# The second routing begun in the last attention steps, and three of 43 expert blocks put under a condition

## The chip, the cores and the metric

One core of one Trainium2 chip runs the whole program in one launch. The metric is the device time of that core in microseconds (us); lower is better. The engines are named as in the profile: PE (TensorE matmul), PEld (its weight loads), DVE (VectorE), ACT (ScalarE), POOL (GpSimd), SP (SyncE).

## The reference

Random-feature attention over 64 heads, and then a mixture of experts in which each token goes to one expert:

```python
B, H, S, Dh = 8, 8, 576, 64           # M = 128 features
proj = x @ omega.T                     # of q and of k
phi  = concat(cos(proj), sin(proj)) / sqrt(M)
kv, z = phi_k.T @ v, sum(phi_k)
attn = (phi_q @ kv) / clamp(phi_q @ z)
x = attn as (N = 4608 tokens, D = 512)
logits = normed(x) @ normed(expert_emb).T / tau   # E = 8 experts
e = argmax(logits); g = softmax(logits)[e]
out[token] = g * (relu(x[token] @ w1[e]) @ w2[e]) # w1 512x1024, w2 1024x512
```

The inputs are the same draw each time. For that draw the argmax sends 1155, 712, 0, 1151, 438, 576, 574 and 2 tokens to the eight experts. Rounded up to blocks of 128 tokens of one expert these are 10 + 6 + 0 + 9 + 4 + 5 + 5 + 1 = 40 blocks. For any input the number is at most 4608 / 128 + 7 = 43, and the kernel before works through 43 blocks always.

## The kernel before, in words

**Attention.** 32 steps n, each one batch and a pair of heads. All engines' queues are written by hand in one loop (the function below the helpers, `for n in range(NS + 1)`), so each engine runs its instructions in the order of the program text. A step n projects and turns into waves the features of k (two steps ahead) and q, sums k features on POOL (`zsum`), multiplies with v, and `num` and `norm` of step n - 1 give rows of x, which go to DRAM (`store_rows`) together with logit sums on POOL (`sums`).

**Routing.** Tokens stand as 36 slots of 128 partitions, 9 slots for a group of two batches. `choose(g)` finds each token's expert on DVE as a one-hot `eq`; `scan` and the two matmuls of `rank` number the tokens of each expert; `starts`, `places` and `places2` make of it a block number and a row in the block; `block_hot` and `row_hot` make one-hots of both, and `invert` (one matmul for a slot) turns them into a list of token numbers by block, which `rows_of` writes as the gather's indices `prm`. `block_experts` gives each block's expert (`eblk`), which PE reads into a register for its weights' addresses.

The first routing (steps 18 to 28) covers the batches 0 to 3 and gives K1 = 11 blocks. The second covers all 36 slots and gives blocks 11 to 42. It can start only when the last attention step has ended, and is spread over blocks j = 0 to 7 by `route_second` (DVE) and `route_second_pe` (PE): `choose` and `scan` at j = 0, `rank` and `starts2` at 1, `places` at 2, `block_hot` at 3, two `row_hot` at 4 and 5 (18 slots each), `invert` and `rows_of` at 6, `block_experts` at 7. A token's number is split there into two parts (`tok_hi`, `tok_lo`), since it doesn't fit in bf16, so `block_hot` has two products and `invert` a right side of 64 columns.

**Blocks.** In iteration j PE runs `hidden(j + 1)` (32 matmuls, L893), then what the routing has for it, then `turn_x(j + 2)` (four transposes, L852) and `result(j)` (8 matmuls of 512 columns, L914). `power` (POOL), `score` and `weigh` (DVE) and `tanh` (ACT) make a block's gate weight. POOL also casts x (`cast`, L806) and issues the scatter of block j (L927) and the gather of block j + 5 (L774). Up to block 7 ACT does PE's evictions alone; later DVE takes a part.

Of the kernel before, what the change touches and what calls it, by code (L numbers as in the profile page):

```python
# [28 lines left out]
def kernel(  # L29
# [19 lines left out]
    P = 128  # L49
# [70 lines left out]
    tok_hi = persist.tile([P, NSLOT], BF16)  # L120
    tok_lo = persist.tile([P, NSLOT], BF16)
    io_p = persist.tile([P, P], BF16)
    io_k = io_p[:, 0:NBLK]
    io_kf = persist.tile([1, NBLK], FP32)
    pref = persist.tile([P, E], BF16)
    tri = persist.tile([P, E, E], FP32)
# [9 lines left out]
    with tc.tile_pool(name="psA", bufs=1, space=PSUM) as psA, tc.tile_pool(  # L136
# [272 lines left out]
        ti = tmpi[:, P : P + NSLOT]  # L409
# [163 lines left out]
        def set_up_routing(n):  # L573
# [6 lines left out]
            elif n == 3:  # L580
                nc.vector.tensor_scalar(ti, tok_i, 63, None, ALU.bitwise_and)
                nc.vector.tensor_copy(tok_lo, ti)
            elif n == 4:
                nc.vector.tensor_scalar(ti, tok_i, 6, None, ALU.arith_shift_right)
                nc.vector.tensor_scalar(tok_hi, ti, 1, None, ALU.add)

        class Arena:
# [3 lines left out]
            def take(self, n, dtype=FP32):  # L591
# [8 lines left out]
                return r if dtype == FP32 else r.bitcast(dtype)[:, 0:n]  # L600

# [59 lines left out]
        def starts2(rk, ns, ar):  # L661
            nc.vector.tensor_copy(sm[:, T0], rk[:, :, ns])
# [7 lines left out]
            nc.vector.tensor_tensor(sm[:, T0], sm[:, T0], sm[:, B1], ALU.subtract)  # L670
            nc.vector.tensor_scalar(sm[:, DOFF], sm[:, T0], float(P), None, ALU.mult)
# [11 lines left out]
        def places2(w, ge, ns, ar):  # L683
            dest = ar.take(ns)
            lo = ar.take(ns, BF16)
            blk = ar.take(ns, BF16)
# [11 lines left out]
        def block_hot(blk, ns, k0, nk, ar):  # L698
            bm = ar.take(ns * nk, BF16).rearrange("p (s k) -> p s k", k=nk)
            rr = ar.take(ns * nk * 2, BF16).rearrange("p (s t k) -> p s t k", t=2, k=nk)  # L700
# [8 lines left out]
        def row_hot(oh, lo, a, b):  # L709
            shp = [P, b - a, P]  # L710
            nc.vector.tensor_tensor(  # L711
# [482 lines left out]
```

## Time and profile before

| what | us |
|---|---|
| median of 3 runs | 521.59 (521.36 to 522.46) |
| the profiled execution, whole | 520.67 |
| its span in the trace | 518.9 |
| attention, to the first matmul of block 0 | 325.5 |
| block 1's first matmul to block 13's (iterations j = 0 to 11) | 331.16 to 395.13 |
| block 13's first matmul to block 42's | 395.13 to 505.00 |
| last scatter issued by | 512.4 |

All numbers of the trace are of the one profiled execution. Busy shares are means over stages with different limits, so stages are read one by one: in the windows table a line is one stretch, with the busy time of each engine in it, the clock that PE was granted (1.00 is full), and what the DMAs moved. A wait is put down to the event that ended it. Line numbers (L893) are those of the kernel before.

### The profile page before, as it was taken

The page shows a single profiled execution, that of the slowest core. Times are in us where ns is not written, and L with a number is a line of the kernel's source. Part 1 is how long each engine was busy: PE and PEld are TensorE (multiplying, and loading weights), DVE is VectorE, ACT ScalarE, POOL GpSimd, SP SyncE. Part 2 cuts the span into 40 slices and gives each one's busy share as a digit, 9 for nine tenths or more (in the row PEclk, how much of TensorE's full clock was granted, in tenths as well). Part 3 has the DMA queues.
Part 4 walks back from the last instruction along what each step waited for, and adds up shares of the span by engine and source line. Part 5 has one row for each costly group of instructions (what it writes and reads, how often), then busy time and mean ns, then how long its engine had stood idle before and what let it go on. Part 6 is the DMA issues. An engine that isn't in the chain of part 4 may idle for free. (4 is left out here: it accounts for less than half of the span.)

```text
span 518.9 us, 19723 instructions
## 1 busy us (share of the span) xinstructions
PE 467.8 (90%) x8073; PEld 381.5 (74%) x8073; DVE 364.6 (70%) x968; ACT 342.9 (66%) x490; POOL 397.4 (77%) x529
## 2 busy tenths in 40 slices
PE   5389999999999999999999988869589999999993
PEld 4378888888887888778888776746457777777771
DVE  2647997677877778879888685569676666666671
ACT  2358988887887887878887775637355554554541
POOL 3549999888787887787778789447768888888872
PEclk9679999999999999999999999989899999999997
DMA  6035899988987988987998876732233334334210
GB/s 188 0 92 135 168 221 193 201 181 195 185 185 178 199 186 170 177 194 161 193 196 167 180 150 134 143 109 97 70 124 124 127 111 136 125 113 150 79 53 1
DMA packets 59113, 75.11 MB, mean 145 GB/s; under 512 B 11398, under 2 KB 38022, under 8 KB 59024
## 3 DMA queue, kind: packets, MB, share of 16 engines
q0 software_dynamic: 19680, 35.83, 34.0%
q1 hardware_dynamic: 39040, 37.93, 27.6%
q8 instruction: 65, 1.06, 0.8%
q14 instruction: 24, 0.20, 0.1%
q10 hardware_dynamic: 304, 0.08, 0.1%
HBM read 73.42 MB, written 20.88 MB: 182 GB/s over the span
## 5 line engine op out<-in xcount | busy, mean ns | idle before, releaser
L893 PEld LDWEIGHTS <-w_sb 128*128 x1376 | 81.0, 98 | 13.4 <-issue 4.2
L893 PE MATMUL ps<-qr,w_sb 128*128 128x128 f16 x1376 | 84.5, 220 | 2.8 <-DVE qr L195 1.7
L914 PE MATMUL ps<-w_sb,cok 128*128 x344 | 82.8, 384 | 0.0
L350 PE MATMUL ps<-kv,siq 128*64 128x73 f32 x1152 | 77.0, 229 | 0.3 <-issue 0.3
L350 PE MATMUL ps<-kv,coq 128*64 128x73 f32 x1152 | 75.5, 226 | 1.4 <-ACT coq L275 1.1
L350 PEld LDWEIGHTS ps<-kv,siq 128*64 128x64 f32 x1152 | 59.4, 135 | 12.2 <-issue 11.2
L287 POOL TENSOR_TENSOR zt<-sik 128x384 f32<-128x384 f32 x32 | 37.0, 1155 | 40.6 <-ACT sik L275 35.2
L774 POOL DMA_INDIRECT xin_all<-rf_x,prm x43 | 47.0, 1093 | 19.6 <-issue 16.3
L350 PEld LDWEIGHTS ps<-kv,coq 128*64 128x64 f32 x1152 | 60.5, 137 | 1.6 <-ACT coq L275 1.2
L263 DVE SCALAR_TENSOR_TENSOR cok<-cok,ps 128x1152 f32<-128x1152 f32 x31 | 42.0, 1354 | 21.7 <-ACT kT L218 20.2
L914 PEld LDWEIGHTS <-cok 128*128 128x128 f16 x344 | 33.2, 99 | 31.6 <-issue 1.6
L228 PE MATMUL ps<-omT,kT 64*128 64x128 f32 x576 | 48.6, 297 | 3.8 <-DVE coq L263 3.5
L275 ACT ACTIVATE cok<-cok,pio 128x1152 f32<-128x1152 f32 x31 | 38.9, 1255 | 17.9 <-DVE cok L269 17.9
L810 ACT ACTIVATE qT<-xin_all 128x512 f16<-128x512 f32 x43 | 27.0, 628 | 31.8 <-DMA xin_all<-rf_x,prm 31.6
L228 PEld LDWEIGHTS ps<-omT,kT 64*128 64x128 f32 x576 | 41.3, 198 | 8.2 <-DVE coq L263 4.3
L263 DVE SCALAR_TENSOR_TENSOR coq<-coq,ps 128x1152 f32<-128x1152 f32 x32 | 43.1, 1346 | 5.0 <-ACT coq L259 5.0
L241 PE MATMUL ps<-qT,omT 32*128 32x288 f32 x512 | 40.6, 431 | 3.2 <-DVE kvT L310 3.0
L275 ACT ACTIVATE siq<-coq 128x1152 f32<-128x1152 f32 x32 | 37.3, 1165 | 8.6 <-DVE coq L263 4.0
L275 ACT ACTIVATE coq<-coq,pio 128x1152 f32<-128x1152 f32 x32 | 40.2, 1256 | 2.7 <-DVE coq L269 2.5
L300 PE MATMUL ps<-sik,v 64*64 64x128 f32 x576 | 36.8, 281 | 5.2 <-DVE coq L263 5.2
L288 POOL TENSOR_TENSOR zt<-zt,sik 128x384 f32<-128x384 f32 x32 | 38.9, 1217 | 2.5
L275 ACT ACTIVATE sik<-cok 128x1152 f32<-128x1152 f32 x31 | 35.8, 1156 | 5.9 <-PE ps L300 5.7
(210 smaller groups left out, 1211.5 us busy)
## 6 DMA issues: line engine op xcount, KB each, us to landing
w_sb<-in_moe_w_dram POOLq DMA_DIRECT2D x32, 512.0 KB
qr<-in_q_dram SPq DMA_DIRECT2D x64, 144.0 KB, 5.2
rf_x<-xb SPq DMA_DIRECT2D x32, 288.0 KB, 6.0
kr<-in_k_dram SPq DMA_DIRECT2D x58, 144.0 KB, 4.0
v<-in_v_dram SPq DMA_DIRECT2D x32, 144.0 KB, 4.2
xin_all<-in_v_dram SPq DMA_DIRECT2D x30, 144.0 KB, 6.9
w_sb<-in_k_dram SPq DMA_DIRECT2D x6, 144.0 KB, 2.8
xin_all<-rf_x,prm POOLq DMA_INDIRECT x43
```

The costliest lines, as they stand in the source:

```text
L228: nc.tensor.matmul(kreg[:, KS[c] * P : KS[c] * P + P], lhsT=t[r0 : r0 + 64, j * P : j * P + P], rhs=omT2[r0 : r0 + 64], start=True, stop=True,
L241: nc.tensor.matmul(qreg[:, g // 2, QW * (g % 2) : QW * (g % 2) + QW], lhsT=omT4[r0 : r0 + 32, b], rhs=t[r0 : r0 + 32].rearrange("p (c b j) ...
L263: nc.vector.scalar_tensor_tensor(out=dst, in0=dst, scalar=CMAGIC, in1=src, op0=ALU.subtract, op1=ALU.subtract)
L275: nc.scalar.activation(st[n][which + nm], t, AF.Sin, bias=pio2 if which == "co" else 0.0, scale=-TWO_PI * SINSC,)
L287: nc.gpsimd.tensor_tensor(zt, t[:, 0:3], t[:, 3:6], ALU.add)
L288: nc.gpsimd.tensor_tensor(zt, zt, t[:, 6:9], ALU.add)
L300: nc.tensor.matmul(kvreg[64 * half : 64 * half + 64, hh], lhsT=d["v"][r0 : r0 + 64, 64 * c : 64 * c + 64], rhs=ph[r0 : r0 + 64, s * P : s ...
L350: nc.tensor.matmul(nm[r0 : r0 + 64, c], lhsT=ph[:, 2 * QW * hh + 64 * c : 2 * QW * hh + 64 * c + 64], rhs=d["kv"][:, hh, half], start=(hal ...
L774: ins = nc.gpsimd.indirect_dma_start(out=t, out_offset=None, in_=x_rows[:], in_offset=bass.IndirectOffsetOnAxis(ap=prm[:, j : j + 1], axis=0),
L810: nc.scalar.activation(late("qT", j % 2, D), xin[j].bitcast(FP32)[:, 0:D], AF.Square, accum_out=gsc[:, j % 4, 0:1],)
L893: nc.tensor.matmul(h_ps[:, f * P : f * P + P], lhsT=weights(k), rhs=d["xT"][:, c * P : c * P + P], start=(c == 0), stop=(c == 3),)
L914: nc.tensor.matmul(y_ps, lhsT=d["hT"][:, c * P : c * P + P], rhs=weights(NW1 + c), start=(c == 0), stop=(c == NW2 - 1),)
```

## The change

1. **Ranks and one-hots early.** The groups 0 to 2 (27 of the 36 slots) are ranked in attention: `scan` on DVE at the end of step 29 and `rank` on PE right behind it; `places_a`, `places_b` and the row one-hot of group 0 at the end of step 30; the row one-hots of groups 1 and 2 at the end of step 31. Row and place don't depend on the last group, only the offset of a block of the second part does. The last group's rank, places and one-hot follow at j = 1 and 2.
2. **A new form of the places.** `pick` multiplies a table of 8 values by `eq` and sums over the experts; offset and block number come for all 36 slots from one `pick` at j = 2. Blocks' order on DVE: `route_second(j)` stands ahead of `score` and `weigh` for j > 0.
3. **One token code.** Token number + 0x400, read as the bits of an fp16 number, replaces the two parts: `block_hot` has one product instead of two, `invert` 32 columns instead of 64, and `rows_of` three DVE instructions instead of four. `invert` and `rows_of` come at j = 5, `block_experts` at j = 6.
4. **Three blocks in a branch.** The loop runs over NMAIN = 40 blocks. `block_experts` also writes the number of blocks (`nbt`); every engine reads it into a register at the end of j = 20, and the last three blocks stand behind `tc.If(nbv > NMAIN)`, one after the other.
5. Buffers: the blocks' hidden rows (`hT`) are in `coq` instead of `cok`, the one-hots in `cok`, and the scratch of the early work in `kT`.

The core of the diff:

```diff
-        def rank(ns, rk):
+        def rank(s0, s1, rk):
+            ns = s1 - s0
             rk = rk[:, 0 : (ns + 1) * E].rearrange("p (e s) -> p e s", e=E)
-            nc.tensor.matmul(rk, lhsT=onesb, rhs=cumx[:, :, 0 : ns + 1], start=True, stop=False)
+            nc.tensor.matmul(rk, lhsT=onesb, rhs=cumx[:, :, s0 : s1 + 1], start=True, stop=False)
             nc.tensor.matmul(
-                rk[:, :, 0:ns], lhsT=sltb, rhs=eq[:, :, 1 : ns + 1], start=False, stop=True
+                rk[:, :, 0:ns], lhsT=sltb, rhs=eq[:, :, 1 + s0 : 1 + s1], start=False, stop=True
             )
             return rk
 
...
+        def slots(s0, s1):
+            return eq[:, :, 1 + s0 : 1 + s1].rearrange("p e s -> p s e")
+
+        def pick(dst, table, s0, s1, ar):
+            t = ar.spare((s1 - s0) * E).rearrange("p (s e) -> p s e", e=E)
+            nc.vector.tensor_tensor(t, table, slots(s0, s1), ALU.mult)
+            nc.vector.tensor_reduce(dst.unsqueeze(2), t, axis=AX.X, op=ALU.add)
+
+        def places_a(rk, s0, s1, ar):
+            ns = s1 - s0
+            d = [ar.take(ns) for _ in range(4)]
+            pick(d[0], rk[:, :, 0:ns].rearrange("p e s -> p s e"), s0, s1, ar)
+            whole(d[1], d[0], -0.49609375)
+            nc.vector.scalar_tensor_tensor(
+                out=p2["lo"][:, s0:s1], in0=d[1], scalar=-float(P), in1=d[0], op0=ALU.mult, op1=ALU.add
+            )
+            return d
+
+        def places_b(d, s0, s1, ar):
+            shp = [P, s1 - s0, E]
+            pick(d[2], bc(sm[:, B1], shp, 1), s0, s1, ar)
+            nc.vector.tensor_tensor(p2["at"][:, s0:s1], d[1], d[2], ALU.add)
+            pick(d[3], bc(sm[:, LIM], shp, 1), s0, s1, ar)
+            nc.vector.tensor_tensor(p2["ge"][:, s0:s1], d[0], d[3], ALU.is_ge)
...
-            nc.vector.tensor_tensor(rr[:, :, 0], bm, bc(tok_hi[:, 0:ns], shp, 2), ALU.mult)
-            nc.vector.tensor_tensor(rr[:, :, 1], bm, bc(tok_lo[:, 0:ns], shp, 2), ALU.mult)
+            nc.vector.tensor_tensor(rr, bm, bc(tokc[:, 0:ns], shp, 2), ALU.mult)
             return rr
...
+                nc.vector.tensor_tensor(
+                    nbt, sm[0:1, ST2, E - 1 : E], sm[0:1, T1, E - 1 : E], ALU.add
+                )
...
+        def early_pe(n):
+            if n == 29:
+                p2["rk"] = rank(0, S3, ROUTE)
+
+        def row_tile():
+            return (
+                pa.tile([P, NCH * P], FP32, tag="cok", name="oh", bufs=2)
+                .bitcast(FP16)
+                .rearrange("p (s m) -> p s m", m=P)
+            )
+
+        def hot(g):
+            s = SG * (g % 2)
+            row_hot(p2["oh"][g // 2][:, s : s + SG], p2["lo"][:, SG * g : SG * g + SG])
+
+        def early_second(n):
+            if n == 29:
+                scan()
+            elif n == 30:
+                ar = p2["ar"] = Arena(pa.tile([P, 5 * P], FP32, tag="kT", name="ar", bufs=1))
+                p2["lo"] = ar.take(NSLOT, FP16)
+                p2["at"] = ar.take(NSLOT)
+                p2["ge"] = ar.take(NSLOT)
+                places_b(places_a(p2["rk"], 0, S3, ar), 0, S3, ar)
+                p2["oh"] = [row_tile()]
+                hot(0)
+            elif n == 31:
+                p2["oh"].append(row_tile())
+                hot(1)
+                hot(2)
...
-                r2["rk"] = r2["a"].take((NSLOT + 1) * E).rearrange("p (e s) -> p e s", e=E)
-                nc.vector.tensor_copy(r2["rk"], r2["ps"])
-                starts2(r2["rk"], NSLOT, r2["a"])
+                starts2(r2["ps"][:, :, SG], r2["a"])
+                d = places_a(r2["ps"], S3, NSLOT, r2["a"])
+                places_b(d, S3, NSLOT, r2["a"])
             elif j == 2:
-                r2["wg"] = places(r2["rk"], NSLOT, r2["a"])
-                r2["blk"], r2["lo"] = places2(*r2["wg"], NSLOT, r2["a"])
+                hot(3)
+                d = r2["a"].take(NSLOT)
+                blk = r2["a"].take(NSLOT, FP16)
+                pick(d, bc(sm[:, DOFF], [P, NSLOT, E], 1), 0, NSLOT, r2["a"])
+                nc.vector.tensor_tensor(d, d, p2["ge"], ALU.mult)
+                nc.vector.tensor_tensor(blk, d, p2["at"], ALU.add)
+                r2["blk"] = blk
             elif j == 3:
                 r2["rr"] = block_hot(r2["blk"], NSLOT, K1, NBLK - K1, r2["a"])
-            elif j == 4:
-                row_hot(r2["oh"][0], r2["lo"][:, 0:18], 0, 18)
             elif j == 5:
-                row_hot(r2["oh"][1], r2["lo"][:, 18:36], 0, 18)
+                rows_of(r2["inv"], K1, NBLK - K1, r2["a"])
             elif j == 6:
-                rows_of(r2["inv"], K1, NBLK - K1, r2["a"])
-            elif j == 7:
                 block_experts(K1, NBLK - K1, True, r2["a"])
...
-        for j in range(NBLK):
+        for j in range(NMAIN):
             eng = "act" if j <= QUIET else "dve"
-            if j + 1 < NBLK:
+            if j + 1 < NMAIN:
                 hidden(j + 1, eng)
             route_second_pe(j)
-            if j + 2 < NBLK:
+            if j > 0:
+                route_second(j)
+            if j + 2 < NMAIN:
                 turn_x(j + 2, eng)
                 power(j + 2)
                 score(j + 2)
-            if j + 3 < NBLK:
+            if j + 3 < NMAIN:
                 cast(j + 3)
                 square(j + 3)
-            if j + 1 < NBLK:
+            if j + 1 < NMAIN:
                 tanh(j + 1)
                 weigh(j + 1)
-            route_second(j)
-            if j + 5 < NBLK and j == 0:
+            if j == 0:
+                route_second(j)
+            if j + 5 < NMAIN and j == 0:
                 gather(j + 5)
             result(j)
-            if j + 5 < NBLK and j > 0:
+            if j + 5 < NMAIN and j > 0:
                 gather(j + 5)
+            if j == 20:
+                nbv = nc.values_load(
+                    nbt[0:1, 0:1], min_val=0, max_val=NBLK,
+                    skip_runtime_bounds_check_because="a count of blocks",
+                )
+
+        with tc.If(nbv > NMAIN):
+            for j in range(NMAIN, NBLK):
+                gather(j)
+            for j in range(NMAIN, NBLK):
+                cast(j)
+                square(j)
+                power(j)
+                score(j)
+                tanh(j)
+                weigh(j)
+                turn_x(j, "dve")
+                expert_of(j)
+                place(j, range(NW1 + NW2))
+                hidden(j, "act")
+                result(j)
```

Left out are the first routing's calls of the changed helpers (`places2` serves it alone now), `row_hot` and `rows_of` with their shorter bodies, and the set-up of the token codes `tokc`. In the changed kernel the row one-hots are at L737, `pick` at L680 and L681, `rows_of` at L750 to L753, a gather at L794, `cast` at L826, `power` at L837, `score` at L843 to L850, `weigh` at L860 to L866, a scatter at L948, the copy of a transposed x at L197, attention's `norm` at L366 to L368, and the branch at L1219.

DVE's queue at the end of step 31, as it was (`gsc` is the scratch of a block's gate, `qr` the transposed x, L364 the first instruction of attention's last `norm`):

```order
L828 TENSOR_SCALAR gsc<-gsc 128x1
L829 RECIPROCAL gsc<-gsc 128x1
L830 TENSOR_SCALAR gsc<-xin_all,gsc 128x8
L195 COPY qr<-ps 128x512
L823 TENSOR_TENSOR ptk<-xin_all,bad 128x1
L827 TENSOR_REDUCE gsc<-xin_all 128x1
```

and as it is now, where `oh` are the row one-hots of the groups 1 and 2:

```order
L848 TENSOR_SCALAR gsc<-gsc 128x1
L849 RECIPROCAL gsc<-gsc 128x1
L850 TENSOR_SCALAR gsc<-xin_all,gsc 128x8
L197 COPY qr<-ps 128x512
L737 TENSOR_TENSOR oh<-io_p,ar 128x1152 x2
L843 TENSOR_TENSOR ptk<-xin_all,bad 128x1
L847 TENSOR_REDUCE gsc<-xin_all 128x1
```

Two row one-hots of 9 slots stand between the copy and the score of block 1.

DVE's queue about iterations 5 and 6 of the blocks, as it was, from a block's `weigh` (L845, L846) to the next block's score:

```order
L845 TENSOR_SCALAR gsc<-gsc 128x1
L846 RECIPROCAL gpos<-gsc 128x1
L711 TENSOR_TENSOR oh<-io_p,xb 128x2304
L823 TENSOR_TENSOR ptk<-xin_all,bad 128x1
L827 TENSOR_REDUCE gsc<-xin_all 128x1
```

and now, ahead of the matching score:

```order
L865 TENSOR_SCALAR gsc<-gsc 128x1
L866 RECIPROCAL gpos<-gsc 128x1
L750 CAST ar<-ps 128x32
L752 TENSOR_SCALAR bad<-ar 128x32
L753 SCALAR_TENSOR_TENSOR prm<-ar,bad 128x32
L843 TENSOR_TENSOR ptk<-xin_all,bad 128x1
```

The one-hot of 18 slots (`oh`, 2304 wide) is gone from here; the inversion's result (`ps`) is read by three DVE instructions an iteration earlier than before.

POOL's queue at the end of the program, as it was (L927 scatters):

```order
L817 TENSOR_TENSOR gsc<-gsc,half_77 128x1
L927 DMA out_dram<-sik,ptk 4608x512
L927 DMA out_dram<-siq,ptk 4608x512
L927 DMA out_dram<-sik,ptk 4608x512
L1189 UNCONDITIONAL_BRANCH
L1189 ISA
```

and now, from the last unconditional scatters on:

```order
L948 DMA out_dram<-sik,ptk 4608x512
L948 DMA out_dram<-siq,ptk 4608x512
L1219 COMPARE_AND_BRANCH
L794 DMA xin_all<-rf_x,prm 128x521 x3
L826 CAST v<-xin_all 128x512
```

The three gathers, casts, powers and scatters of the blocks 40 to 42 now follow the comparison; if it fails, POOL's queue jumps to a second piece of code that ends the same way as the body.

## Rows read from the trace of the kernel before

**Rows 1.** Busy times of the page, and PE in its 40 slices.

```profile
PE 467.8 (90%) x8073; PEld 381.5 (74%) x8073; DVE 364.6 (70%) x968; ACT 342.9 (66%) x490; POOL 397.4 (77%) x529
...
PE   5389999999999999999999988869589999999993
```

**Rows 2.** Windows table, steady blocks: engine busy us (instructions), then clock, DMA share, GB/s.

```profile
395.13:505.00 109.87, 109.34 (x1277) 81.85 (x1276) 72.19 (x378) 57.35 (x143) 92.76 (x116) 1.00 0.36 114
```

**Rows 3.** Windows table, same columns: blocks j = 1, 2, 5, 6, 7 and 8.

```profile
334.90:344.21 9.31, 5.13 (x47) 3.22 (x46) 6.30 (x31) 3.23 (x8) 4.65 (x7) 0.89 0.59 144
344.21:349.45 5.24, 4.59 (x45) 3.48 (x44) 2.85 (x17) 2.42 (x5) 3.22 (x4) 0.86 0.30 95
...
356.94:362.21 5.27, 4.01 (x45) 2.83 (x44) 5.17 (x10) 3.17 (x7) 5.07 (x4) 1.00 0.28 82
362.21:373.95 11.74, 6.45 (x81) 4.71 (x80) 8.64 (x30) 3.28 (x8) 8.67 (x8) 0.85 0.28 92
373.95:378.35 4.40, 3.90 (x45) 2.79 (x44) 1.15 (x10) 2.42 (x5) 2.90 (x4) 1.00 0.20 67
378.35:383.93 5.58, 3.90 (x45) 2.78 (x45) 4.97 (x21) 3.23 (x9) 3.79 (x6) 1.00 0.41 130
```

**Rows 4.** Waits of PE between 331 and 396 us: total, times, longest.

```profile
PE ps L634 <- DVE cumx L630: 4.2, 1, 4.2
PE ps L893 <- DVE qr L195: 1.7, 1, 1.7
PE ps L852 <- POOL v L806: 1.3, 1, 1.3
```

**Rows 5.** Groups by form, 331.16 to 395.13 us: the inversion on PE.

```profile
L718 PE MATMUL ps<-ar,oh 128*128 128x64 bf16 x36 | 1.8, 218 | 5.3 <-DVE oh L711 5.3
```

**Rows 6.** Windows table near the end, same columns; the last is GB/s.

```profile
500.80:504.00 3.20, 3.20 (x43) 2.58 (x42) 2.35 (x14) 1.38 (x3) 2.29 (x4) 1.00 0.11 40
504.00:508.00 4.00, 4.00 (x44) 2.79 (x43) 2.74 (x14) 1.38 (x3) 1.13 (x2) 1.00 0.04 5
508.00:512.00 4.00, 2.40 (x12) 0.88 (x9) 0.95 (x7) 1.37 (x2) 1.56 (x2) 1.00 0.01 0
```

**Rows 7.** Source line L711, row one-hots on DVE: ns min/median/max.

```profile
L711 DVE TENSOR_TENSOR w_sb<-io_p,w_sb x2: 1347/1348/1348, 261.7 to 270.6; 128x1152 bf16<-128x1152 bf16 x2
```

**Rows 8.** Timeline of DVE, second routing: start, us, instruction.

```profile
353.16 0.67 DVE L688 TENSOR_TENSOR xb<-xb,eq 128x288 f32<-128x288 f32 x1
353.86 0.45 DVE L691 TENSOR_REDUCE xb<-xb 128x36 f32<-128x288 f32 x1
...
359.55 1.76 DVE L706 TENSOR_TENSOR ar<-xb,tok_lo 128x1152 bf16<-128x1152 bf16 x1
...
362.99 2.61 DVE L711 TENSOR_TENSOR oh<-io_p,xb 128x2304 bf16<-128x2304 bf16 x1
```

**Rows 9.** Timeline of POOL in the same place.

```profile
364.06 1.96 POOL L817 TENSOR_TENSOR gsc<-gsc,half 128x1 f32<-128x1 f32 x1
```

**Rows 10.** Source line L817, the power on POOL: ns min/median/max.

```profile
L817 POOL TENSOR_TENSOR gsc<-gsc,half x43: 572/584/1960, 323.7 to 503.5; 128x1 f32<-128x1 f32 x43
```

**Rows 11.** Timeline of DVE, steps 30 to 32: idle time before in brackets.

```profile
322.96 0.43 DVE L195 COPY qr<-ps 128x512 f16<-128x512 f16 x1 [5.31 <-PE ps L852]
...
331.30 0.15 DVE L828 TENSOR_SCALAR gsc<-gsc 128x1 f32<-128x1 f32 x1 [2.62 <-POOL gsc L817]
```

**Rows 12.** Timeline of POOL, step 31: the gather of block 3.

```profile
328.99 1.11 POOL L774 DMA_INDIRECT xin_all<-rf_x,prm  x1 [4.63 <-issue]
```

**Rows 13.** Source line L867, register loads on PE: ns min/median/max.

```profile
L867 PEldq TENSOR_LOAD <-eblk x43: 297/301/916, 318.2 to 502.3; - x43
```

**Rows 14.** Source line L1189, the program's end: ns min/median/max, first and last start.

```profile
L1189 SPq EVENT_SEMAPHORE  x11: 17/28/14996, 498.4 to 518.8; - x11
...
L1189 POOLq DRAIN  x3: 51/103/6913, 511.2 to 518.6; - x3
```

**Rows 15.** Timeline of POOL: the last scatter.

```profile
511.40 0.97 POOL L927 DMA_INDIRECT out_dram<-sik,ptk  x1 [0.76 <-ACT sik L926]
```

More of the change, by code (lines that the diff above doesn't have):

```diff
@@ L119 @@
     eblk = persist.tile([1, NBLK], I32)
[L120 to L122 removed]
+    TOK0 = 0x400
+    tokc = persist.tile([P, NSLOT], FP16)
+    nbt = persist.tile([1, 1], I32)
+    io_p = persist.tile([P, P], FP16)
     io_k = io_p[:, 0:NBLK]
@@ L580, in set_up_routing @@
             elif n == 3:
[L581 to L585, printed above, removed]
+                nc.vector.tensor_scalar(tokc.bitcast(I16), tok_i, float(TOK0), None, ALU.add)
         class Arena:
@@ L600, in take, with spare @@
                 return r if dtype == FP32 else r.bitcast(dtype)[:, 0:n]
+            def spare(self, n):
+                if not hasattr(self, "sp"):
+                    self.sp = self.take(n)
+                return self.sp[:, 0:n]
         def bc(ap, shape, axis):
@@ L684, in places2 @@
             dest = ar.take(ns)
-            lo = ar.take(ns, BF16)
-            blk = ar.take(ns, BF16)
+            lo = ar.take(ns, FP16)
+            blk = ar.take(ns, FP16)
             nc.vector.tensor_tensor(w, w, ge, ALU.add)
@@ L727, in rows_of @@
         def rows_of(inv, k0, nk, ar):
[L728 removed]
+            t = ar.take(nk, FP16)
             bd = bad[:, k0 : k0 + nk]
             nc.vector.tensor_copy(t, inv)
[L731 removed]
+            tok = t.bitcast(I16)
+            nc.vector.tensor_scalar(bd, tok, float(TOK0), 200000.0, ALU.is_lt, ALU.mult)
             nc.vector.scalar_tensor_tensor(
[L733 to L737 removed]
+                out=prm[:, k0 : k0 + nk], in0=tok, scalar=-float(TOK0), in1=bd, op0=ALU.add, op1=ALU.add
             )
@@ L910, in result @@
             y_ps = bank(3 + 4 * (j % 2))
-            if j + 2 < NBLK:
+            more = NMAIN if j < NMAIN else 0
+            if j + 2 < more:
                 expert_of(j + 2)
@@ L920, in result @@
                 )
-                if j + 2 < NBLK and c < 6:
+                if j + 2 < more and c < 6:
                     place(j + 2, range(6 * c, min(6 * c + 6, NW1)))
-                if j + 1 < NBLK and c >= 6:
+                if j + 1 < more and c >= 6:
                     place(j + 1, range(NW1 + 6 * (c - 6), min(NW1 + 6 * (c - 5), NW1 + NW2)))
@@ L949, in route_pe @@
             if m == 2:
-                r1["ps"] = rank(S1, ROUTE)
+                r1["ps"] = rank(0, S1, ROUTE)
             elif m == 8:
@@ L1064 @@
                 route_first(n - n1)
+            if not last:
+                early_second(n)
+            early_pe(n)
             if here:
@@ L1091, in route_second_pe @@
             if j == 1:
-                r2["ps"] = rank(NSLOT, bank(6 - 4 * (j % 2)))
-            elif j == 6:
+                r2["ps"] = rank(S3, NSLOT, bank(6 - 4 * (j % 2)))
+            elif j == 5:
                 r2["inv"] = invert(
-                    lambda s: r2["oh"][s // 18][:, s % 18],
+                    lambda s: p2["oh"][s // S1][:, s % S1],
                     r2["rr"], NSLOT, NBLK - K1, bank(6 - 4 * (j % 2)),
@@ L1100, in route_second @@
             if j == 0:
-                oh = [
-                    pa.tile([P, NCH * P], FP32, tag="coq", name="oh", bufs=2)
-                    .bitcast(BF16)
-                    .rearrange("p (s m) -> p s m", m=P)
-                    for _ in range(2)
-                ]
-                r2["oh"] = oh
-                r2["a"] = Arena(
-                    *[
-                        pa.tile([P, NCH, 2 * (W - 1)], FP32, tag="xb", name="xb", bufs=2).rearrange(
-                            "p c w -> p (c w)"
-                        )
-                        for _ in range(2)
-                    ],
-                    pa.tile([P, NCH * P], FP32, tag="cok", name="ar", bufs=2),
+                r2["a"] = Arena(
+                    pa.tile([P, NCH * P], FP32, tag="coq", name="ar", bufs=2),
+                    pa.tile([P, NCH, 2 * (W - 1)], FP32, tag="xb", name="xb", bufs=2).rearrange(
+                        "p c w -> p (c w)"
+                    ),
                 )
+                r2["a"].spare(NSLOT * E)
                 choose(NGRP - 1)
```

52 lines of the change are left out of this document (20 added, 32 removed).

## The prediction

> **What bounds the kernel now.** I read the page's busy shares first: PE is busy 90% of the span, and in the 40 slices its digit is 9 nearly throughout, except for a dip of seven slices a little past the middle [rows 1]. That dip is where attention ends and the second routing runs. So the next view is the windows table, cut at the first matmul of each block's `hidden`. From block 13 to block 42 it shows 29 blocks in 109.87 us, 109.34 of them PE busy at clock 1.00, with POOL at 92.76 as the next busiest [rows 2]. A steady block thus costs 109.87 / 29 = 3.79 us, and PE alone sets it. Against that price I hold the iterations in which the second routing runs [rows 3]. Over 3.79 they lose 5.52 us at j = 1, 1.45 at 2, 1.48 at 5, 7.95 at 6, 0.61 at 7 and 1.79 at 8. PE's waits name the causes: `rank` waits 4.2 us for DVE's scan at j = 1, a transpose waits 1.3 us for POOL's cast at j = 5, and a `hidden` waits 1.7 us for DVE's copy at j = 8 [rows 4]. The groups by form give the one at j = 6: 36 inversion matmuls, 1.8 us busy, stand behind 5.3 us of waiting for the row one-hot L711 [rows 5].
>
> **Three blocks fewer.** First, are there only 40 blocks with tokens? The reference says so for this draw, and the trace agrees. Near the end the DMAs move 40 GB/s x 3.20 us = 128 kB, then 5 x 4.00 = 20 kB, then nothing [rows 6]. A scattered row is 512 x 4 bytes, so 128 kB is 62 rows, the remainder of an expert with 574 = 4 x 128 + 62 tokens. After it comes the block of two tokens, and the last three scatters carry nothing. The comparison fails and three blocks are skipped: 3 x 3.79 = **-11.4 us**. They are the end of the steady stretch, whose work PE does at full clock, so nothing covers them.
>
> **The second routing's stalls.** At j = 6 the wait for the row one-hot goes: the change makes three of four groups in attention and the fourth at j = 2, so the inversion (now at j = 5) waits only for the product of `block_hot`, made at j = 3. The inversion's own 1.8 us [rows 5] stay. That gives 7.95 - 1.8 = 6.15. The 0.61 of j = 7 is the tail of the same jam. The 1.79 of j = 8 is the wait for a copy on DVE [rows 4], queued there behind `block_experts`; the change puts that one iteration earlier, where ACT still evicts alone. Together 6.15 + 0.61 + 1.79 = **-8.5**. I keep the 5.52 of j = 1 (choose and scan of the last group still come after attention and `rank` still waits for them) and the 1.45 of j = 2 and 1.48 of j = 5, since DVE's list work now goes ahead of the gate's work and only moves. Bounds: -4.3 if half of it comes back as waits for DVE at j = 2 to 5, -10.0 if the wait of j = 5 goes too.
>
> **Early work in attention.** Step 29's scan and rank stand where PE later waits for other engines, and I cost them at nothing. If that cover fails, `rank`'s wait delays the queries' projection behind it; the upper bound of this term has room for that. At the end of step 30 DVE gets three `pick` of 216 elements, five short instructions and a row one-hot of 1152, which took 1.35 us in the first routing [rows 7]. A product of 288 took 0.67 and its sum 0.45 [rows 8], so at 216 a pick is an estimated 0.50 + 0.34; with the short ones at 0.15 to 0.2, by the nearest row [rows 11], the sum is 2.5 + 0.9 + 1.35 = 4.8, at most 5.7 with the prices of 288. DVE stood idle 5.31 there [rows 11]. So this costs -0.5 to +0.4: nothing. At the end of step 31 two one-hots (2.70) come ahead of the score of block 1, in an idle stretch of 2.62 [rows 11]: +0.1. What isn't hidden is POOL. While the 18-slot one-hot ran from 362.99 for 2.61 us [rows 8], the power on POOL, started at 364.06, took 1.96 us [rows 9] instead of its median 0.58 [rows 10]. In step 31 the same power, a gather (issue at 328.99) [rows 12] and a cast lie beside the one-hots, and DVE's score waits for that power [rows 11]. I add 1.96 - 0.58 = 1.4 once, and 0.5 for part of the cast's delay (its bound is the 1.35 of one one-hot). Sum: **+2.0**, between 0 and +4 (two slow powers and a whole 1.35).
>
> [...]
>
> **Small edits.** Each of the five engines reads a register at the end of j = 20. The same kind of load for the experts took 0.30 us on PE's queue, 0.92 at most [rows 13]; there are 43 of these now, ahead of work that PE's list already holds. POOL and DVE have 17 and 38 us of slack in the steady stretch [rows 2]. Zero, at most +0.9. A narrower inversion, one product less (1.76 us of DVE [rows 8]) and one DVE instruction less in `rows_of` are off PE's path: zero, and part of the -8.5.
>
> **The end.** Behind block 39 every engine compares and jumps. Before, POOL's last scatter is issued at 511.40 + 0.97 = 512.4 [rows 15], while its final drain takes 6.9 us from 511.2 and SP's last waits reach to the span's end [rows 14]. The jump and one more semaphore instruction come ahead of that drain. No row shows a branch over a body. The nearest short thing is a register load, 0.3 [rows 13]; the far one is the whole drain, 6.9. I take **+1.5**, nearer the short end, since a comparison moves no data and the scatters' landing can hide part; below, 0, since nothing is taken away here but the blocks already counted.
>
> [...]
>
> **Sum.** -11.4 - 8.5 + 2.0 + 0 + 1.5 = -16.4. The profiled execution took 520.67 us (span 518.9, and 1.8 around it), so 504.3; the median of the runs, 521.59, lies 0.9 above that execution, so 505.2. I say **505.0**.
>
> **Rivals.**
> 1. *POOL is held up throughout.* For: the 1.96 us power. Against: the median of 43 is 0.58, so most escape. Every one-hot and product then delays POOL's cast, and PE waits for it as at j = 5. The routing gains only 4.3 and the early work costs 4: 505.2 + 4.2 + 2.0 = 511.4. Chance 0.15.
> 2. *The end costs a second drain.* For: the failing side raises a semaphore after waits on all scatter queues. Against: only one drain of 6.9 stands in the trace. +6.9 in place of 1.5: 510.6. Chance 0.10.
> 3. *Everything pays.* Early work and branch cost nothing and the wait of j = 5 goes: 505.2 - 2.0 - 1.5 - 1.5 = 500.2. Chance 0.10. For it: DVE's idle stretches are long enough.
> 4. *The branch is taken.* If the count that the chip computes is over 40, three blocks run one after another, with gather, cast, transposes and both products in a row and nothing beside them. One such block costs at least 3.79 and at most the 11.74 of the worst iteration [rows 3]; I take twice the steady price, 7.6. Then -11.4 becomes 3 x 7.6 - 11.4 = +11.4: 505.2 + 22.8 = 528.0, slower than before. It decides from 41 blocks on. Against: the byte counts of the last three scatters. Chance 0.02.
>
> **How the numbers follow.** The forecast keeps 0.63, with its own range 501 to 509 from the terms' bounds. A measurement of this kernel can tell about 0.2%, 1.0 us, from no change. Every case but the fourth lies over 10 us below the time before; I leave 0.01 for no change and 0.03 for slower. The range takes in rivals 1 to 3 but for their outer halves: 500 to 511.5.
>
> **What would show it.** In the profile after: steady blocks still near 3.79, and one fewer stretch of three; PE's wait for the inversion gone or under 1 us and the iterations 5 to 8 near 4 to 5.6; `rank` still waiting some 4 us; the first block's start within 2 us of 325.5 and DVE's score of block 1 waiting longer for POOL's power; the time from the last scatter's issue to the span's end, now 518.9 - 512.4 = 6.5, at about 8. The prediction is wrong if the iterations after the second routing keep a wait of 4 us or more, if the end grows by 5 or more, or if 43 blocks still run.

## The result, and the profile after

The changed kernel takes 502.19 us (median of 4 runs, 500.04 to 504.27), the kernel before 521.97 (521.36 to 522.46). The ratio is 0.962 with a 95% interval of 0.957 to 0.967, so 19.8 us are gone where 16.6 were forecast (505.0 against the 521.59 known then). The profiled execution, the shortest of the four, took 500.04 us, with a span of 498.2. Ratios, here and below, leave out runs that lie over 1.5% above the shortest run of the same kernel.

The page of the changed kernel, its busy times and PE in 40 slices:

```profile
PE 454.5 (91%) x7943; PEld 371.9 (75%) x7943; DVE 361.8 (73%) x941; ACT 339.5 (68%) x475; POOL 387.7 (78%) x517
...
PE   5389999999999999999999997895999999999992
```

The dip of seven slices [rows 1] has shrunk to four. The windows table, cut at the first matmul of each block's `hidden`, shows j = 1, 2, 4, 5, 6 and then 25 steady blocks (columns as in [rows 3]; `...` marks left-out lines, here and in every cut below):

```profile
334.80:345.47 10.67, 5.66 (x47) 3.37 (x46) 7.76 (x39) 3.65 (x10) 5.49 (x7) 0.84 0.58 135
345.47:349.21 3.74, 3.74 (x45) 2.79 (x44) 3.43 (x18) 2.97 (x7) 2.25 (x2) 1.00 0.20 74
...
353.44:358.25 4.81, 3.99 (x45) 2.83 (x44) 4.17 (x15) 3.32 (x9) 4.30 (x5) 1.00 0.33 111
358.25:362.89 4.64, 4.64 (x81) 3.69 (x80) 2.08 (x14) 3.19 (x7) 4.11 (x6) 1.00 0.44 148
362.89:366.63 3.74, 3.74 (x46) 2.79 (x44) 3.17 (x14) 2.98 (x7) 2.98 (x5) 1.00 0.46 146
...
389.62:483.63 94.01, 93.80 (x1101) 70.05 (x1100) 63.54 (x330) 51.57 (x126) 79.92 (x100) 1.00 0.39 123
```

The worst iteration of before, 11.74 us at j = 6, is a plain 3.74 now. The inversion stands at j = 5 and PE does not wait for it: the groups by form give 36 matmuls in 1.1 us with no idle time before them (to compare with [rows 5]):

```profile
L742 PE MATMUL ps<-xb,oh 128*128 128x32 f16 x36 | 1.1, 176 | 0.0
```

PE's waits between 331 and 396 us (to compare with [rows 4]):

```profile
PE ps L637 <- DVE cumx L632: 5.0, 1, 5.0
PE ps L872 <- POOL v L826: 1.3, 3, 0.8
```

The wait for a row one-hot and the one for the copy at j = 8 are gone; `rank`'s wait for the scan grew from 4.2 to 5.0, and the iteration j = 1 from 9.31 to 10.67. Between the two profiled executions the account is: first matmul of block 1 -0.1 us (331.16 to 331.06); iterations 1 to 9 -9.7 (52.76 to 43.04); the rest up to the last `hidden` -11.6 (31 iterations in 117.34, 28 in 105.79); behind it +0.6 (13.9 to 14.5). Together -20.7, the difference of the spans.

The source line of the program's end bears on the last of these:

```profile
L1264 POOLq DRAIN  x3: 50/103/5215, 492.1 to 497.9; - x3
```

and the line of the condition, where POOL raises a semaphore ahead of that drain:

```profile
L1219 POOLq COMPARE_BRANCH  x1: 50/50/50, 489.8 to 489.8; - x1
L1219 POOLq INC_SWDGE_SEM  x1: 1447/1447/1447, 490.6 to 490.6; - x1
```

The drain's 6.9 [rows 14] are 1.45 + 5.2 now.

### The profile page after: what moved, and what is told of

Read it like the earlier page. It is cut to its first block, busy times and chain, and to the rows that moved or that the text cites. A ratio compares the mean times of both kernels' runs of the same rounds, so it can differ in the third digit from the quotient of the medians.

```text
span 498.2 us, 19379 instructions
## 1 busy us (share of the span) xinstructions
PE 454.5 (91%) x7943; PEld 371.9 (75%) x7943; DVE 361.8 (73%) x941; ACT 339.5 (68%) x475; POOL 387.7 (78%) x517
## 5 line engine op out<-in xcount | busy, mean ns | idle before, releaser
L913 PEld LDWEIGHTS <-w_sb 128*128 x1280 | 74.7, 98 | 9.9 <-issue 1.3
L352 PE MATMUL ps<-kv,siq 128*64 128x73 f32 x1152 | 78.3, 231 | 0.5 <-issue 0.5
L913 PE MATMUL ps<-qr,w_sb 128*128 128x128 f16 x1280 | 78.0, 219 | 0.2 <-DVE qr L197 0.2
L352 PE MATMUL ps<-kv,coq 128*64 128x73 f32 x1152 | 76.6, 229 | 1.0 <-ACT coq L277 1.0
L935 PE MATMUL ps<-w_sb,coq 128*128 x320 | 77.0, 385 | 0.0
L289 POOL TENSOR_TENSOR zt<-sik 128x384 f32<-128x384 f32 x32 | 38.0, 1186 | 36.3 <-ACT sik L277 31.1
L794 POOL DMA_INDIRECT xin_all<-rf_x,prm x40 | 43.9, 1098 | 19.2 <-issue 11.3
L935 PEld LDWEIGHTS <-coq 128*128 128x128 f16 x320 | 30.5, 99 | 29.5 <-issue 1.6
L830 ACT ACTIVATE qT<-xin_all 128x512 f16<-128x512 f32 x40 | 25.1, 628 | 34.7 <-DMA xin_all<-rf_x,prm 34.7
L289 POOL TENSOR_TENSOR zt<-cok 128x384 f32<-128x384 f32 x32 | 36.8, 1151 | 4.5 <-ACT cok L277 2.3
```

The lines of the kernel that those rows point to most:

```text
L289: nc.gpsimd.tensor_tensor(zt, t[:, 0:3], t[:, 3:6], ALU.add)
L352: nc.tensor.matmul(nm[r0 : r0 + 64, c], lhsT=ph[:, 2 * QW * hh + 64 * c : 2 * QW * hh + 64 * c + 64], rhs=d["kv"][:, hh, half], start=(hal ...
L794: ins = nc.gpsimd.indirect_dma_start(out=t, out_offset=None, in_=x_rows[:], in_offset=bass.IndirectOffsetOnAxis(ap=prm[:, j : j + 1], axis=0),
L830: nc.scalar.activation(late("qT", j % 2, D), xin[j].bitcast(FP32)[:, 0:D], AF.Square, accum_out=gsc[:, j % 4, 0:1],)
L913: nc.tensor.matmul(h_ps[:, f * P : f * P + P], lhsT=weights(k), rhs=d["xT"][:, c * P : c * P + P], start=(c == 0), stop=(c == 3),)
L935: nc.tensor.matmul(y_ps, lhsT=d["hT"][:, c * P : c * P + P], rhs=weights(NW1 + c), start=(c == 0), stop=(c == NW2 - 1),)
```

## The experiments

They ran in four groups (e1 to e4, e5 to e8, e9 to e11, e12), each on its own chip, with runs of the kernel before beside it (medians 531.02, 528.42, 525.34 and 527.02 us; single runs from 519.65 to 535.94). The changed kernel itself was run again only in the third group, as e9. The kernel before varies there by up to 15 us on one chip, and attention takes longer: in the profiles of the experiments block 0 starts at 327 to 337 us, not at 325.5. For e1, e7 and e9 the runs themselves are given, not a ratio. So the verdicts rest on this table too, from the starts of `hidden` in one profile each (us): iteration j runs from `hidden(j + 1)` to `hidden(j + 2)`, and the tail from the last `hidden` to the span's end.

| kernel | j = 1 | j = 4 | j = 5 | j = 6 | sum j = 1 to 9 | mean from j = 12 | tail |
|---|---|---|---|---|---|---|---|
| before | 9.31 | 3.75 | 5.27 | 11.74 | 52.76 | 3.79 | 13.9 |
| the change | 10.67 | 4.81 | 4.64 | 3.74 | 43.04 | 3.76 | 14.5 |
| e1 branch alone | 8.95 | 3.74 | 5.27 | 11.87 | 52.74 | 3.82 | 14.5 |
| e2 routing alone | 10.66 | 4.38 | 5.54 | 4.26 | 45.38 | 3.79 | 13.9 |
| e3 no branch | 10.30 | 3.94 | 5.60 | 3.73 | 43.70 | 3.79 | 13.4 |
| e5 rank later | 4.75 | 3.76 | 10.69 | 5.70 | 46.05 | 4.16 | 14.5 |
| e6 one-hots after | 8.61 | 7.49 | 5.57 | 3.74 | 45.27 | 4.19 | 14.5 |
| e7 one-hots late | 9.18 | 3.73 | 4.62 | 6.14 | 45.43 | 4.15 | 14.5 |
| e8 one-hots twice | 12.50 | 4.39 | 5.58 | 3.74 | 45.85 | 4.14 | 14.5 |
| e9 change again | 10.54 | 4.87 | 5.56 | 4.26 | 44.71 | 4.13 | 14.5 |
| e10 loads late | 11.11 | 4.90 | 5.58 | 4.27 | 45.88 | 3.78 | 14.5 |
| e11 both | 5.00 | 3.75 | 6.59 | 6.62 | 44.10 | 3.79 | 14.5 |
| e12 spread | 4.73 | 4.71 | 3.73 | 10.54 | 46.59 | 3.78 | 14.5 |

The change, e2, e3, e9, e10 and e4 (45.41, not in the table) have the same second routing, and their sums for j = 1 to 9 reach from 43.0 to 45.9, with a mean of 44.7. So a difference of under 3 us between two single sums shows nothing, and the first profile of the change had the lowest of the six.

### The parts by themselves: e1, e2, e3

e1 puts the branch on the kernel before:

```diff
-        for j in range(NBLK):
+        for j in range(NMAIN):
...
+        with tc.If(nbv > NMAIN):
+            for j in range(NMAIN, NBLK):
```

> The kernel before with the loop over 40 blocks and the three last in the branch, the second routing untouched. By the traces, three blocks of 3.74 us go (-11.2) and the tail behind the last scatter grows by 0.7 us: 10.5 less than the kernel before, about 511.5 us, with the 11.7 us iteration j = 6 still there. If the two parts lean on each other (the branch pays only where the early routing has shortened the iterations) it gains less than 9.

Six runs from 515.81 to 528.86, median 523.85: 7.2 below the 531.02 beside it, not 10.5. The two shortest, the profiled one among them, have a mean of 517.6, and that is 10.5 below the 528.1 of the runs of the kernel before that the ratios use. In the profile the routing's 52.74 us are as before, three blocks are gone and the tail is 14.5. So the parts hold in these two runs; the other four take 523.8 to 528.9, and no profile shows why.

e2 takes the changed kernel with all 43 blocks, no loads and no branch:

```diff
-    NMAIN = NBLK - 3
+    NMAIN = NBLK
...
-            if j == 20:
-                nbv = nc.values_load(
```

> The changed kernel with all 43 blocks in the loop and neither register loads nor branch. By the traces the routing alone gives 9.8 us for j = 1 to 8 and nothing in attention: about 512.2 us. By the forecast's terms (-8.5 and +2.0) it gives 6.5: 515.5 us.

521.58 us, ratio 0.987 (0.980 to 0.994): 6.9 of 528.1 us, with an interval of 3 to 10. In the profile the iterations 1 to 9 take 45.38, 7.4 less than in the kernel before. Both lie nearer to the forecast's 6.5 than to the 9.8 of the first profile, though the interval holds both.

e3 drops loads, condition and the three blocks (same diff, but for NMAIN).

> The changed kernel without the condition, the five register loads and the three blocks behind it (leaves out blocks 40 to 42 altogether). If the 0.7 us that the trace shows behind the last scatter are the branch's whole price: 0.7 us faster than the changed kernel, some 501.5 us. If the loads or the jump cost more before the end, or make its runs spread over 4 us: 2 us or more faster, with runs within 1 us of each other. Forecast's term: 1.5.

510.98 us, ratio 0.967 (0.960 to 0.974). On the chip of e2 that is 10.6 less than e2: the three blocks. The tail is 13.4 instead of 14.5, so the branch costs 1.1 us there. Whether the whole is 0.7 or over 2 us faster than the changed kernel stays open, since that was not run on this chip. The runs do not lie within 1 us of each other: they reach from 508.93 to 514.6, without any load or branch.

### The branch taken: e4

```diff
-        with tc.If(nbv > NMAIN):
+        with tc.If(nbv > NMAIN - 1):
```

> The changed kernel with the condition at 39, so that the three blocks run though they hold no tokens. The rival of the forecast priced a block behind the branch at 7.6 us, 22.8 for three: about 525 us. If gathers, casts and transposes of the three overlap, 15 us: 517. If each pays the worst iteration's 11.7: 537.

555.24 us, ratio 1.048 (1.040 to 1.057), slower than before. From block 39's `hidden` on, the three blocks start 14.88, 10.88 and 10.58 us apart: 36.3 for three, not 22.8. The windows table over the last 19.9 us, from 4.8 us ahead of the last block's `hidden`, shows an almost idle chip and PE at a mean clock of 0.68:

```profile
533.00:552.90 19.90, 6.86 (x44) 4.67 (x44) 1.80 (x10) 2.61 (x6) 3.27 (x4) 0.68 0.01 1
```

The change thus buys its 11 us for draws with at most 40 blocks and pays for any with more (the 4.8% of this trial hold also the slower blocks that come behind the register loads, below).

### Where the one-hots stand: e6, e7, e8

e6 moves the two of step 31 to j = 2:

```diff
                 p2["oh"].append(row_tile())
-                hot(1)
-                hot(2)
...
             elif j == 2:
+                hot(1)
+                hot(2)
                 hot(3)
```

> The changed kernel with the row one-hots of groups 1 and 2 at j = 2, beside group 3's, instead of in step 31. If they cost nothing in step 31 and something later: 0 to 3 us slower, with the rank's wait still 5 us. If, as forecast, they cost 2 us in step 31 (POOL's power and gather held up): the wait at j = 1 falls back to 4.2, and the kernel is about 1 us faster unless the three one-hots then delay the cast of block 5.

521.55 us, ratio 0.986 (0.981 to 0.991). PE's waits from 331 to 385 us:

```profile
PE ps L637 <- DVE cumx L632: 3.9, 1, 3.9
PE ps L872 <- POOL v L826: 3.5, 1, 3.5
```

`rank` waits 3.9 us, near the 4.2 of before [rows 4], and j = 1 is 1.9 us shorter than in e9 (10.54). But POOL's cast is 3.5 us late at j = 4, an iteration of 7.49. The sum, 45.27, lies within the spread of the unmoved routing: the two one-hots cost some 2 us in step 31, and no less shows where they stand now.

e8 computes them twice:

```diff
                 hot(1)
                 hot(2)
+                hot(1)
+                hot(2)
```

> The changed kernel with the two row one-hots of step 31 computed twice, one after the other (2.6 us more on DVE). If DVE has no slack left there and the score of block 1, the last logits and the scan stand behind it: about 2.6 us slower. If POOL's hold is what counts, more than that, 4 us. If idle time covers it, nothing.

520.47 us, ratio 0.986 (0.981 to 0.991). `rank`'s wait grows by the second pair's time, less what idle time takes:

```profile
PE ps L637 <- DVE cumx L632: 6.9, 1, 6.9
```

j = 1 takes 12.50 us, 2.0 more than in e9, for 2.6 more on DVE. So the chain from these one-hots over the score of block 1 to the scan has little idle time left at this place, and what they cost is about their own time on DVE; the 4 us that were expected of a hold of POOL on top did not come.

e7 moves all four back to j = 4 and 5 and the inversion to 6:

```diff
...
+            elif j == 4:
+                hot(0)
+                hot(1)
             elif j == 5:
+                hot(2)
+                hot(3)
+            elif j == 6:
                 rows_of(r2["inv"], K1, NBLK - K1, r2["a"])
-            elif j == 6:
+            elif j == 7:
...
```

> The changed kernel with all four row one-hots at j = 4 and 5, inversion and rows at 6 and experts at 7, as in the kernel before; early rank, places and the token code stay. If it is the place of the one-hots that made the iteration of 11.7 us, that comes back: 6 us slower than the changed kernel, 508. If the one code, the shorter inversion and the order of DVE's work made the gain, it stays within 2 us: 504.

Six runs from 505.72 to 525.49, median 518.9. The iteration with the inversion takes 6.14 us, not 11.7, and j = 1 falls to 9.18; the sum, 45.43, lies within the spread of the unmoved routing. So where the one-hots stand is worth less than these profiles can tell. What shortened the iteration of 11.74 is in what e7 keeps: the one token code with its narrower inversion, the early ranks and places, or DVE's list work ahead of the score. These three were not taken apart.

### The register loads: e9, e10

In the profiles of e4 to e8, all with loads at j = 20, the blocks from j = 23 on take 4.3 to 4.6 us. In e2 and e3, without loads, they do not. The first profile of the change and that of e1 have the loads too and show 3.74 to 3.8 there. e9 is the changed kernel once more; e10 moves the loads:

```diff
-            if j == 20:
+            if j == 36:
                 nbv = nc.values_load(
```

> The changed kernel itself, beside the two that follow. In the profiles of four kernels with the register loads at j = 20 the blocks from about j = 22 on take 4.4 to 4.5 us instead of 3.74; in both without loads they don't. If the loads set this off, the same shows here in most runs: 8 to 10 us above the 500 to 504 first measured where it does, and a gain of only 2 % over the kernel before. If it belongs to the chip or to chance, this kernel and the next agree.

> The changed kernel with the five register loads at the end of j = 36, behind the last gather, instead of j = 20. If the loads at j = 20 set off the slow blocks: 5 to 10 us faster than the changed kernel on the same chip, blocks 12 to 37 at 3.74 to 3.79 us, PE without waits for DVE's copy. If not: the same within 1 us, as the forecast priced the loads at nothing wherever they stand.

e9's runs are 504.48, 513.95, 514.22, 515.13, 515.59 and 516.55 us; e10's lie between 505.53 and 509.63, median 506.28, ratio 0.967 (0.963 to 0.972) to the kernel before. Moving five loads of 0.47 to 0.55 us each in e9 gives 8.4 us by the medians, and the runs lie within 4.1 us of each other instead of 12.1. The one short run of e9 is no longer than those of e10, so the move does not shorten the best run; it makes most runs like it. Over all profiles, six of the eight with loads at j = 20 have the slower blocks (e9's 4.3 to 4.6 us among them) and none of the six without them or with late ones. PE's waits from 400 to 500 us in e9:

```profile
PE ps L913 <- DVE qr L197: 7.4, 14, 0.7
```

In e10 there is none in that stretch. The timeline of e10 (DVE and POOL; start, us) shows a block as it should be:

```profile
442.65 0.67 DVE L925 TENSOR_SCALAR coq<-ps 128x512 f16<-128x512 f32 x1
443.23 1.04 POOL L794 DMA_INDIRECT xin_all<-rf_x,prm  x1 [0.30 <-issue]
443.24 0.41 DVE L197 COPY qr<-ps 128x512 f16<-128x512 f16 x1
```

DVE's relu (L925) starts 0.58 us ahead of the gather's issue on POOL (L794), and the copy of x (L197) starts together with the gather. In ten blocks of e10 in a row, from 431 to 466 us, the relu is 0.57 to 0.66 ahead, and from 400 to 480 us POOL's power is all that DVE waits for. In e9 the load on DVE itself, and the gather behind it:

```profile
L1214 POOLq TENSOR_LOAD <-nbt x1: 511/511/511, 427.8 to 427.8; - x1
L1214 DVEq TENSOR_LOAD <-nbt x1: 545/545/545, 427.9 to 427.9; - x1
```

and the timeline that follows (rows of DVE and POOL, the last of PE):

```profile
428.58 0.69 DVE L925 TENSOR_SCALAR coq<-ps 128x512 f16<-128x512 f32 x1 [0.48 <-issue]
428.58 1.04 POOL L794 DMA_INDIRECT xin_all<-rf_x,prm  x1 [0.30 <-issue]
...
433.09 0.42 DVE L197 COPY qr<-ps 128x512 f16<-128x512 f16 x1 [0.66 <-PE ps L872]
...
436.17 0.69 DVE L925 TENSOR_SCALAR coq<-ps 128x512 f16<-128x512 f32 x1 [0.54 <-PE ps L872]
436.19 1.04 POOL L794 DMA_INDIRECT xin_all<-rf_x,prm  x1 [0.30 <-DMA xin_all<-rf_x,prm]
...
437.61 0.42 DVE L197 COPY qr<-ps 128x512 f16<-128x512 f16 x1 [0.75 <-PE ps L935]
...
440.05 1.04 POOL L794 DMA_INDIRECT xin_all<-rf_x,prm  x1 [0.30 <-DVE gpos L866]
...
441.58 0.69 DVE L925 TENSOR_SCALAR coq<-ps 128x512 f16<-128x512 f32 x1 [1.59 <-PE ps L872]
...
442.18 0.41 DVE L197 COPY qr<-ps 128x512 f16<-128x512 f16 x1
...
442.65 1.95 PE L913 MATMUL ps<-qr,w_sb 128*128 128x128 f16 x32 [0.66 <-DVE qr L197]
```

DVE reaches the relu 0.48 us late behind its load, and relu and gather now start together. One block on, the copy is 0.66 us late, though the relu is ahead again. Two blocks on, the copy starts 0.38 us after the gather's end (437.23), and from the next block the relu itself, 0.45 to 0.52 after the gather's end in twelve blocks in a row. The view puts these waits down to PE, but PE's transposes had started 1.7 us before the relu in this block and 1.5 in the next, while the distance to the gather stays the same. The late copy holds `hidden`, PE runs later, and the next gather again comes first: the state keeps itself up to the last gather. Behind that one it ends:

```profile
488.76 1.04 POOL L794 DMA_INDIRECT xin_all<-rf_x,prm  x1 [0.30 <-issue]
...
490.26 0.69 DVE L925 TENSOR_SCALAR coq<-ps 128x512 f16<-128x512 f32 x1 [1.73 <-PE ps L872]
...
492.96 0.57 POOL L837 TENSOR_TENSOR gsc<-gsc,half 128x1 f32<-128x1 f32 x1
493.32 0.69 DVE L925 TENSOR_SCALAR coq<-ps 128x512 f16<-128x512 f32 x1 [0.34 <-PE ps L913]
493.50 0.60 POOL L826 CAST v<-xin_all 128x512 f16<-128x512 f32 x1
```

Power and cast are still there, the gather is not, the relu starts 0.20 us after the first transpose, and the two iterations take 3.73 and 3.74; the five other profiles with the slower blocks end the same way, with two iterations of 3.73 and 3.74 behind the last gather, and in e6 three relus from 442 us on stand at the same distance to the gather, 0.47 to 0.50 us. So it is with the gather that DVE's delay comes and goes. Why a gather on POOL should delay DVE no run shows.

### A better version? e5, e11, e12

The largest stall left is `rank`'s 5.0 us at j = 1. e5 puts it behind the result of j = 2 and every later step one iteration later:

```diff
...
+            if j == 2:
+                r2["ps"] = rank(S3, NSLOT, bank(2))
+                route_second(j)
...
```

> The changed kernel with the last group's rank behind the result of j = 2 instead of behind the hidden layer of j = 1, and every later step of the routing one iteration later (inversion at j = 6, as in the kernel before). If PE's 5.0 us wait for the scan at j = 1 is idle time that other work can fill, the 10.7 us iteration falls to about 4 to 5, and the whole by 4 to 6 us: about 497. If the wait only moves (to the inversion, which then waits for DVE's block one-hots, or to POOL), it stays within 1.5 us of the changed kernel.

520.85 us, ratio 0.983 (0.978 to 0.988). j = 1 falls to 4.75, and j = 5 rises to 10.69, by a wait for a cast on POOL:

```profile
PE ps L872 <- POOL v L826: 6.9, 5, 5.4
```

behind which POOL's gather waited 5.0 us for DVE's gate weight. The wait moved; the sum, 46.05, is no lower than that of the unmoved routing.

e11 combines late loads, the later rank, and DVE's list work behind the gate weight:

```diff
-            if j > 0:
+            if j > 4:
                 route_second(j)
...
-            if j == 0:
+            if j in (0, 3, 4):
                 route_second(j)
```

> Loads late as in the one before, the rank of the last group behind the result of j = 2, and DVE's list work of j = 2 to 4 behind the gate weights of its iteration, the inversion at j = 6. If the wait that the first trial of a later rank moved to POOL's cast at j = 5 (5.4 us, behind 8 us of list work ahead of the gate weight) came from DVE's order, the iterations 1 to 8 lose 4 us less than the changed kernel's: 3 to 5 us faster than with late loads alone. If the last group's chain on DVE is what bounds it, the wait appears again at the inversion: within 1 us.

506.07 us, ratio 0.962 (0.956 to 0.968), on the chip of e10: the same by the medians, where 3 to 5 us were hoped for. The sum, 44.10, is within the spread of the unmoved routing: j = 1 takes 5.00, and j = 5 and 6 take 6.6 each.

e12 cuts the list work into four pieces:

```diff
+            elif j == 2:
+                r2["rk"] = r2["a"].take((SG + 1) * E).rearrange("p (e s) -> p e s", e=E)
+                nc.vector.tensor_copy(r2["rk"], r2["ps"])
...
+            elif j == 5:
+                r2["rr"] = block_hot(r2["blk"], NSLOT, K1, NBLK - K1, r2["a"])
```

> Loads late, the last group's rank behind the hidden layer of j = 2, and DVE's list work in four pieces of 2 to 3 us, each behind the gate weight of j = 2, 3, 4 and 5 (the rank is copied out of its bank first), inversion at j = 6. DVE waits some 2.3 us for POOL's power in each block there, so pieces of that size should cost nothing: the iterations 1 to 9 then take about 38 us, where the kernel with late loads took 45.9 and the second trial of a later rank 44.1, and the ratio to the kernel before falls from 0.967 to about 0.953. If the last group's chain on DVE bounds the stretch however it is cut, the wait comes back at the inversion, with 44 us and a ratio of 0.962 or more.

515.21 us, ratio 0.978 (0.969 to 0.987). The iterations up to 5 are cheap, and the inversion waits:

```profile
PE ps L742 <- DVE xb L732: 3.8, 1, 3.8
```

The 2.3 us that DVE waits for POOL's power are those of one block of e11 (2.31 at 353.03 us); in the five scores behind it, beside the list work, DVE shows no wait for the power. The sum, 46.59, is nowhere near the 38 hoped for. That fits the rival, by which the last group's chain on DVE bounds the stretch wherever PE meets it; no trial shortened that chain, so it is argued, not shown. The version to keep is e10, which differs from the change in one number.

## Why the forecast held, step by step

**Three blocks: right.** -11.4 was forecast; three steady blocks of 3.74 are -11.2, and e3 stands 10.6 below e2. No more than 40 blocks ran. (Of the 20 kB that the forecast read as the block of two tokens [rows 6], 4 kB are those rows, and the other 16 are one packet of the instruction queue, by the DMA view from 504 to 508 us; the count does not hang on it.)

**The second routing's stalls: right in size, wrong in reason.** The forecast had -8.5, from j = 6, 7 and 8. These three gave -10.5 in the profile (21.72 to 11.21), with the inversion now at j = 5, and j = 2 to 5, that included, gave 0.6 more. With the early work's +2.0 the forecast's net is -6.5; the sum of j = 1 to 9, which holds both, fell by 9.7 in the first profile and by 8.1 in the mean of the six with this routing, and the runs of e2 give 6.9. So the size is right within what the runs can tell. What failed is the reason, "the wait for the row one-hot goes: the change makes three of four groups in attention". With all four back at j = 4 and 5, e7 has no such wait either. Which of the other parts of the routing removed it stays open.

**Early work in attention: right in size, wrong in place.** +2.0 was forecast at the end of attention. Block 0 starts at 325.48, against 325.54. The cost appeared behind it, as a longer wait of `rank`: +1.4 at j = 1, 1.9 by e6, 2.0 for a second pair by e8. The mechanism was to be a power on POOL of 1.96 us, for which DVE's score of block 1 would wait longer. The longest power is 1.05 now, and that score waits 0.50 for it, not 2.62 as before [rows 11], for the one-hots fill the time. The cost is DVE's own time ahead of the scan. On POOL the gather beside the one-hots is the longer one, as its timeline shows (1.11 before [rows 12]):

```profile
328.89 1.81 POOL L794 DMA_INDIRECT xin_all<-rf_x,prm  x1 [5.79 <-issue]
330.70 0.75 POOL L826 CAST v<-xin_all 128x512 f16<-128x512 f32 x1
331.42 0.58 POOL L837 TENSOR_TENSOR gsc<-gsc,half 128x1 f32<-128x1 f32 x1
```

**Waits of j = 1, 2 and 5: kept, and half right.** j = 1 stayed and grew. j = 2's 1.45 went in this profile: its clock had been 0.86 [rows 3] and is 1.00 now, while that of j = 1 fell to 0.84. In e2, e4 and e10, with the same routing, j = 2 takes 4.5 us, and its 32 matmuls of `hidden` 2.66 to 2.68 where they take 1.95 in this profile and 2.63 in the one before, so most of this is luck of the one execution. j = 5's wait went, and smaller ones came at j = 3 and 4.

**The end: +1.5 forecast, +0.6 in the profile,** 1.1 against e3. From the last scatter's issue to the span's end it is 7.1 us instead of 6.5, not 8. Rival 2's second drain did not come.

**Register loads: the term that was wrong.** They were costed at "Zero, at most +0.9". In the first profile they do cost 0.5 (3.88 and 4.11 us in the two iterations where they stand), but on the chip of e9 five of six runs lie 8 to 10 us above e10's median, and the sixth does not. Had the first four runs done so too, 8.4 us more would have made 510.6, outside the forecast's own 501 to 509. That they did not is luck. Why one run tips over and another does not stays open. The 4 us of spread in the first four runs need no loads: e3 has none and spreads over 5.7. The slack of POOL and DVE in a steady block (busy for 79.9 and 63.5 of 94.0 us in the first profile) was no cover in e9 for a load of 0.55 us behind which the gather came ahead of the relu.

**The rivals.** The profiled execution, 500.04 us, is nearly rival 3's 500.2, and the median, 502.19, lies between that and the forecast. Rival 3's way it was not: the early work did cost 1.4 to 2, and in this profile the routing gave more. Rival 1's holding of POOL by DVE would be the 0.7 us of the gather in step 31; nothing like a halved gain came of it. Rival 4's price was too low, 22.8 us for what took 36.3, and the draw did not ask for it.

## What to carry to other kernels

The steady loop of this kernel, bound by PE, has two rhythms, 3.74 us a block and 4.3 to 4.6; behind the loads at j = 20 (0.55 us on DVE in e9) it stayed in the slower one up to the last gather in six of eight profiles. So one-time work is better put where the loop's neighbours no longer meet, here behind the last gather (e10). Price a move by the chain that it joins, not by the idle time at its old or new place: every trial to move `rank`'s wait met waits further on, for POOL's cast (5.4 us in e5, 1.8 in e11) or for a DVE product (3.8 us in e12), and the sums for j = 1 to 9, 44.1 to 46.6 us, show no shorter stretch than the 43.0 to 45.9 of the unmoved routing. And one profile does not speak for a kernel: the first one of this change showed the loads at half a microsecond, and five of six later runs at some eight; and the same second routing took 43.0 to 45.9 us in six profiles.

## What the runs showed of the hardware that was not expected

- Where a gather's issue on POOL (1.04 us) comes ahead of a DVE relu out of PSUM, 512 wide to fp16, the relu starts 0.45 to 0.52 us after the gather's end (twelve blocks of e9), 1.45 to 1.71 after PE's first transpose; with the last gather gone, 0.20 after it. Where the relu starts 0.57 us or more ahead, neither was late in ten blocks of e10, though in e9 one copy was 0.66 late all the same. Blocks with the late relu take 4.3 to 4.6 us instead of 3.74.
- The three blocks behind the taken branch in e4 start 10.6 to 14.9 us apart, from block 39's `hidden` on, 2.8 to 4 times a steady one of 3.74.
- In the changed kernel's profile (L1219), with the condition failing, the comparison takes 45 to 72 ns on four engines and 1.18 us on PE's queue, and the semaphore on POOL 1.45 us.
